# Tying scores and results to TensorE's order by halves of four heads in a gated linear attention and mixture-of-experts kernel

## The chip, the cores and the metric

The kernel runs on one core of a Trainium2 chip, in float32. The metric is the device time of one execution in microseconds (us). The kernel before takes 552.49 us (median of three runs, 552.18 to 552.93).

## What is computed

Two blocks follow one another. The first is a gated linear attention with a complex, per-channel decay; its output is laid out as 3072 rows of 384 numbers. The second sends each row to one of eight experts (two matrix products with a relu between them) and scales the result. Cut to what matters:

```
# attention: B, H, S, D = 4, 8, 768, 48
for t in range(S):
    S_re, S_im = a[t] * (S_re, S_im)  (complex)      # per-channel decay, |a| capped at 0.999
    S_re += outer(k[t], v[t])
    y[t] = q[t] @ S_re
x = y as (B*S, H*D) = (3072, 384)

# experts: E, F = 8, 1024
e = argmax(x @ w_gate)                               # one expert for a row
out = softmax weight of e * (relu(x @ w1[e]) @ w2[e])
```

## The kernel before

The attention is done in chunks of 128 time steps. There are 24 chunks: six steps in time (`s`), and for each of them the four batches (`b`). Two chunks make a unit `u`. With the sums of the logarithms of the decay and of its angles inside a chunk, the recurrence becomes matrix products. For one chunk `g`, and for each of its eight heads:

- `rotated` makes Q and K (128 time steps x 96: cosine and sine part of 48 channels) on VectorE.
- Q and K are transposed on TensorE into `tp` (PSUM, two buffers) and copied to `qt` and `kt`, by ScalarE and VectorE, four heads at a time.
- `at` = scores (128 x 128 for a head); VectorE multiplies them with the triangular mask into `am`.
- `y` = V x `am` plus (from the second time step on) carried state `G` x `qt`. These products have 64 output rows for a head. Two heads are put beside one another, `z` = 0 and `z` = 1, on the lower and the upper 64 partitions of the result.
- `dk` = K x V, what the chunk adds to the state.
- then `y` is copied, transposed (`tpx`), and the router's logits (`lt`, `lp`) are computed.

All matmuls are issued through one helper, so that the profile shows them at one line (L81); the transposes of Q and K are at L504.

```
    def scores(g):
        u, c = divmod(g, U)
        s, b = divmod(g, B)
        Q, K = rotated(u, c, "Q"), rotated(u, c, "K")
        qts, ats = [], []
        for hg in range(H // 4):                       # two halves of four heads
            kq = []
            for nm, X in (("qt", Q), ("kt", K)):
                tp = psT.tile([P, 4, P], FP, tag="tp", name="tp")
                for j in range(4):
                    nc.tensor.transpose(out=tp[0:DD, j], in_=X[:, hg * 4 + j], identity=ident)
                t = ch.tile([P, 4, P], FP, tag=nm, name=nm, bufs=4 if nm == "qt" else 2)
                copy(nm == "qt" or hg == 1, t[0:DD], tp[0:DD])     # True: ScalarE, False: VectorE
                kq.append(t)
            at = psA.tile([P, 4, P], FP, tag="at", name="at")      # one buffer
            for j in range(4):
                mm(at[:, j], kq[1][0:DD, j], kq[0][0:DD, j])
            am = ch.tile([P, 4, P], FP, tag="am", name="am", bufs=4)
            nc.vector.tensor_tensor(out=am, in0=at, in1=bc(tri, 1, 4), op=OP.mult)
            ...
        if s < CB - 1:
            dk = ...
            for h in range(H):
                mm(dk[0:DD, h], K[:, h], T["v", u][:, c, h, 0:D])

    def outputs(g):
        ...
        y = psY.tile([P, HP, P], FP, tag="y", name="y")            # one buffer
        for i in range(HP):                                        # four pairs of heads
            for z in range(2):
                hg, j = divmod(2 * i + z, 4)
                mm(y[z * DP : (z + 1) * DP, i], V[:, 2 * i + z], ats[hg][:, j], True, s == 0)
            if s > 0:
                for z in range(2):
                    hg, j = divmod(2 * i + z, 4)
                    mm(y[z * DP : (z + 1) * DP, i], G[0:DD, 2 * i + z], qts[hg][0:DD, j], False, True)
        ...                       # new state; copy of y to xt (ScalarE); transposes tpx; logits lt, lp

    for u in range(NU + 1):
        ...                       # decay and angle sums (csl, cst) of unit u
        for c in range(U):
            g = (u - 1) * U + c
            if g >= 0:
                scores(g)
            if u < NU:
                decayed(u, c)
            if g > 0:
                outputs(g - 1)    # one chunk behind the scores
            ...                   # routing
    outputs(NT - 1)
```

This text does not fix the order in which an engine executes. A scheduler orders each engine's instructions when the program is built, with the dependencies as its limits. The helper `queue(ins, before)` adds a dependency that costs no semaphore: it only fixes that `ins` comes after `before` in the order.

After the attention (at about 278 us) come the experts: for each one, `hps` = x W1, relu, `yps` = h W2.

Of the kernel before, what the change touches and what calls it, by code (L numbers as in the profile page):

```python
# [10 lines left out]
FP = mybir.dt.float32  # L11
# [3 lines left out]
OP = mybir.AluOpType  # L15
# [5 lines left out]
P = 128  # L21
# [8 lines left out]
def bc(ap, axis, n):  # L30

    shape = list(ap.shape)
    shape.insert(axis, n)
    return ap[tuple([slice(None)] * axis + [None])].to_broadcast(shape)
# [3 lines left out]
def kernel(  # L38
# [12 lines left out]
    nc = tc.nc  # L51
    B, H, S, D = q.shape
    DD = 2 * D
# [4 lines left out]
    NT = N // P  # L58
    CB = S // P
    U = 2  # L60
# [14 lines left out]
    DP = 64  # L75
    HP = H // 2
# [3 lines left out]
    def mm(o, lhsT, rhs, start=True, stop=True):  # L80
        return nc.tensor.matmul(o, lhsT=lhsT, rhs=rhs, start=start, stop=stop, skip_group_check=True)  # L81

    def copy(i, o, in_):
        (nc.scalar.copy if i % 2 else nc.vector.tensor_copy)(out=o, in_=in_)  # L84
# [7 lines left out]
    def const(shape, name, dt=FP):  # L92
        return cp.tile(shape, dt, name=name)

    ident = const([P, P], "ident")
    make_identity(nc, ident)
    tri = const([P, P], "tri")
# [21 lines left out]
    gbuf = [const([P, H, DP], f"G{i}") for i in range(B)]  # L119
# [39 lines left out]
    T, W_T = {"put": []}, {}  # L159

    def queue(ins, before):

        tc.add_manual_dep(ins.ins, before.ins.name, NOSYNC, reason="queue order")
        return ins
# [55 lines left out]
    ch = att.enter_context(tc.tile_pool(name="ch", bufs=2))  # L220
    psM = att.enter_context(tc.tile_pool(name="psM", bufs=1, space=PSUM))
    psT = att.enter_context(tc.tile_pool(name="psT", bufs=2, space=PSUM))
    psA = att.enter_context(tc.tile_pool(name="psA", bufs=1, space=PSUM))
    psY = att.enter_context(tc.tile_pool(name="psY", bufs=1, space=PSUM))
    psB = att.enter_context(tc.tile_pool(name="psB", bufs=1, space=PSUM))
    psD = att.enter_context(tc.tile_pool(name="psD", bufs=1, space=PSUM))
# [47 lines left out]
    def load_a(u):  # L274
        load(u, (("ar", a_re), ("ai", a_im)))
# [131 lines left out]
    def rotated(u, c, nm):  # L407
        t = ch.tile([P, H, 2, D], FP, tag=nm, name=nm)
        e = bc(T.pop((nm, u, c)), 2, 2)
        nc.vector.tensor_tensor(out=t, in0=T["CS", u][:, c * H : (c + 1) * H], in1=e, op=OP.mult)  # L410
        return t.rearrange("p h a d -> p h (a d)")
# [78 lines left out]

        return [lambda i=i: put(i) for i in range(n)] + ([last] if end else [])

    def scores(g):

        u, c = divmod(g, U)
        s, b = divmod(g, B)
        Q, K = rotated(u, c, "Q"), rotated(u, c, "K")
        qts, ats = [], []
        for hg in range(H // 4):
            kq = []  # L500
            for nm, X in (("qt", Q), ("kt", K)):
                tp = psT.tile([P, 4, P], FP, tag="tp", name="tp")
                for j in range(4):
                    nc.tensor.transpose(out=tp[0:DD, j], in_=X[:, hg * 4 + j], identity=ident)  # L504
                t = ch.tile([P, 4, P], FP, tag=nm, name=nm, bufs=4 if nm == "qt" else 2)
                copy(nm == "qt" or hg == 1, t[0:DD], tp[0:DD])
                kq.append(t)
            at = psA.tile([P, 4, P], FP, tag="at", name="at")
            for j in range(4):
                mm(at[:, j], kq[1][0:DD, j], kq[0][0:DD, j])  # L510
            am = ch.tile([P, 4, P], FP, tag="am", name="am", bufs=4)
            nc.vector.tensor_tensor(out=am, in0=at, in1=bc(tri, 1, 4), op=OP.mult)  # L512
            qts.append(kq[0])
            ats.append(am)
        if s < CB - 1:
            dk = psD.tile([P, H, D], FP, tag="dk", padded_shape=[P, 8, 64], name="dk")
            for h in range(H):
                mm(dk[0:DD, h], K[:, h], T["v", u][:, c, h, 0:D])
            T["dk", g] = dk
        T["s", g] = qts, ats  # L520

    def outputs(g):

        u, c = divmod(g, U)
        s, b = divmod(g, B)
        qts, ats = T.pop(("s", g))
        V, G = T["v", u][:, c], gbuf[b]
        y = psY.tile([P, HP, P], FP, tag="y", name="y")
        for i in range(HP):
            for z in range(2):  # L530
                hg, j = divmod(2 * i + z, 4)
                mm(y[z * DP : (z + 1) * DP, i], V[:, 2 * i + z], ats[hg][:, j], True, s == 0)
            if s > 0:
                for z in range(2):
                    hg, j = divmod(2 * i + z, 4)
                    mm(y[z * DP : (z + 1) * DP, i], G[0:DD, 2 * i + z], qts[hg][0:DD, j], False, True)
        if s < CB - 1:
            t = ch.tile([P, H, D], FP, tag="t", name="t")
            if s == 0:
                nc.scalar.copy(out=t[0:DD], in_=T["dk", g][0:DD])  # L540
            else:
                nc.vector.tensor_tensor(out=t[0:DD], in0=T["dk", g][0:DD], in1=G[0:DD, :, 0:D], op=OP.add)
            if b == B - 1:
                decay_total(s)
            T["t", b] = t
            if b == B - 1:
                for i in range(B):
                    M = bc(T["M", s][0:DD, i], 2, D)
                    (nc.vector.tensor_tensor(out=gbuf[i][0:DD, :, 0:D], in0=T["t", i][0:DD], in1=M, op=OP.mult))
        xt = xl.tile([P, HP, P], FP, tag="xt", name="xt")  # L550
        nc.scalar.copy(out=xt, in_=y)
        tp = psB.tile([P, HP, 2, DP], FP, tag="tp", name="tpx")
        for i in range(HP):
            nc.tensor.transpose(out=tp[:, i].rearrange("p z d -> p (z d)"), in_=xt[:, i], identity=ident)  # L554
        if b == 0:
            T["x", g] = T["x"] = xl.tile([P, GR, XW], FP, tag="x", name="x", bufs=3)
        T["copied"] = nc.scalar.copy(
            out=T["x"][:, b, :DM].rearrange("p (i z d) -> p i z d", z=2, d=D), in_=tp[:, :, :, 0:D]
        )
        logits(xt, g)  # L560
# [24 lines left out]
    for z in range(2):  # L585
        nc.sync.dma_start(
            out=wg[z * DP : z * DP + D, :, 0:E],
            in_=w_gate.rearrange("(i z d) e -> z d i e", z=2, d=D)[z],
# [14 lines left out]
    for u in range(NU + 1):  # L603
        if 0 < u < NU:
            load_qkv(u)
        for i in range(NS // (P * BL)):
            if 2 + i * 2 // (NS // (P * BL)) == u:
                blank(i)

        if u < NU:  # L610
            steps = decay_steps(u + 1)[0] if u + 1 < NU else []
            own = [lambda c=c: decay_sums(u, c) for c in range(U)]
            if u == 0:
                steps = steps[:2] + own + steps[2:]
            else:
                steps = steps[:1] + own[:1] + steps[1:3] + own[1:] + steps[3:]
            table("natural_log_exp_and_others")
            for i, f in enumerate(steps):
                f()
                if i == 1:  # L620
                    carry_angle(u)
            for f in T.pop("chosen", []):
                f()
            for c in range(U):
                angle_sums(u, c)
            table("trig_and_small")
            if 0 < u < NU - 1:
                decay_angle(u + 1)
            rotation(u)
            if u == 0:  # L630
                decay_angle(1)
            if u == NU - 1:
                while T["put"]:
                    place()
                experts_at(range(1), True)
                load_w(0, range(KD + KF // 2))
                own0 = gather(0, 0, [P] * (FIRST // P))
        if u < NU:
            place()
        for f in T.pop("route", []):  # L640
            T["put"] += f()
        for c in range(U):
            g = (u - 1) * U + c
            if g >= 0:
                scores(g)
            if u < NU:
                decayed(u, c)
            if g > 0:
                outputs(g - 1)

            n = {NT - GR: GR, NT - U: U}.get(g)
            if n:
                if n == GR:
                    queue(table("natural_log_exp_and_others"), T["copied"])
                choose(g - n, n)()
                T["put"] += route(g - n, n)
                while T["put"]:
                    place()
        for _ in range(2 if u >= NU - 2 else 1):
            place()  # L660
        if u > 2 and u % 2 and u < NU - 1:

            j = (u - 3) * U
            T["chosen"] = [choose(j, GR)]
            T["route"] = [lambda j=j: route(j, GR)]
        if u + 2 < NU:
            load_a(u + 2)
    outputs(NT - 1)
    choose(NT - U, U)()
    for f in route(NT - U, U):  # L670
# [343 lines left out]
```

## Time and profile before

| | |
|---|---|
| time, median of three | 552.49 us |
| span of the profiled execution | 551.8 us |
| TensorE busy (PE) | 535.6 us |
| VectorE busy (DVE) | 272.0 us |
| ScalarE busy (ACT) | 279.7 us |
| first matmul of the experts (hps) | 278.5 us |

In the profile PE stands for TensorE's matmuls, PEld for its weight loads, DVE for VectorE, ACT for ScalarE, POOL for GpSimd. A float32 matmul that is no transpose shows as two records of equal shape, so "x8" of `at` is four matmuls. The ends of matmuls are modelled and overlap; what a group of matmuls costs is therefore read from its start to the start of the next group.

### The profile page before, as it was taken

How to read it: one execution, taken by the hardware profiler on the slowest of the kernel's cores; microseconds unless marked ns; L12 is line 12 of the kernel's file. 1: busy time of each engine (PE TensorE's matmuls, PEld its weight loads, DVE VectorE, ACT ScalarE, POOL GpSimd, SP SyncE). 2: the span in 40 equal slices, each digit the busy share in tenths (PEclk: the TensorE clock that was granted, in tenths of full speed). 3: DMA queues.
4: the chain of work that ended last, by engine and by line, in shares of the span. 5: the costliest groups of instructions: out<-in, count | busy, mean ns of one | idle time of the engine just before them, and what ended most of it. 6: DMA issues, size and time to landing. Idle time of an engine off the chain costs nothing.

```text
span 551.8 us, 8779 instructions
## 1 busy us (share of the span) xinstructions
PE 535.6 (97%) x3310; PEld 369.7 (67%) x3310; DVE 272.0 (49%) x640; ACT 279.7 (51%) x473; POOL 128.5 (23%) x148
## 2 busy tenths in 40 slices
PE   8899999999999999999999999999999999999995
PEld 6777688778778878778776655555555555565553
DVE  3757788978888887877551212121404032210110
ACT  7867877877776886744310112534343351615200
POOL 2110111141241140210222000605234160514301
PEclk9959999999999999999999999999999999999998
DMA  9999954918754633461114996472944819370001
GB/s 186 187 259 236 262 94 88 182 52 145 129 131 88 121 84 58 105 224 18 43 44 113 309 359 160 136 194 121 281 137 163 240 47 280 128 255 15 25 4 42
DMA packets 163566, 79.32 MB, mean 144 GB/s; under 512 B 144896, under 2 KB 156861, under 8 KB 162619
## 3 DMA queue, kind: packets, MB, share of 16 engines
q1 hardware_dynamic: 158651, 69.04, 51.6%
q0 software_dynamic: 4864, 9.63, 5.0%
q8 instruction: 28, 0.46, 0.4%
q14 instruction: 23, 0.19, 0.1%
HBM read 63.30 MB, written 15.46 MB: 143 GB/s over the span
## 4 chain that ended last, share of the span: by engine, by line
PE 84%; DMA 6%; DVE 3%; ACT 3%; issue 3%; SPq 0%; POOL 0%; POOLq 0%; DVEq 0%; ACTq 0%
PE hps L81 23%; PE yps L81 22%; PE y L81 9%; PE at L81 7%; PE tp L504 7%; PE dk L81 5%; PE cst L81 3%; PE csl L81 3%; DMA ai<-in_a_im_dram 2%; PE tpx L554 2%; DMA xs<-x,slot 1%; PE lt L81 1%; DMA ai<-c 1%; DMA c<-ai 1%; ACT R L230 1%
## 5 line engine op out<-in xcount | busy, mean ns | idle before, releaser
L81 PE MATMUL yps<-w2t,ht 128*128 128x384 f32 (+6 forms) x464 | 135.1, 487 | 0.0
L81 PE MATMUL hps<-xt,w1t 128*128 128x256 f32 (+8 forms) x432 | 133.9, 469 | 0.3 <-DVE xt L708 0.3
L81 PEld LDWEIGHTS hps<-xt,w1t 128*128 128x128 f32 x432 | 80.0, 190 | 52.8 <-issue 25.2
L81 PEld LDWEIGHTS yps<-w2t,ht 128*128 128x128 f32 (+6 forms) x464 | 75.8, 177 | 56.8 <-issue 6.9
L742 ACT ACTIVATE ht<-hps 128x256 f32<-128x256 f32 (+8 forms) x36 | 17.0, 472 | 118.5 <-PE hps L81 117.5
L759 DVE TENSOR_SCALAR y<-yps,gi 128x384 f32<-128x384 f32 (+2 forms) x24 | 14.7, 615 | 107.6 <-PE yps L81 107.6
L722 POOL DMA_INDIRECT out_dram<-y,gi x29 | 28.2, 974 | 122.6 <-DVE y L759 86.5
L81 PE MATMUL at<-qt,kt 96*128 96x128 f32 x384 | 54.9, 286 | 0.9 <-DVE kt L84 0.9
L746 DVE TENSOR_SCALAR ht<-hps 128x256 f32<-128x256 f32 (+8 forms) x36 | 19.2, 532 | 70.9 <-PE hps L81 70.8
L81 PEld LDWEIGHTS at<-qt,kt 96*128 96x128 f32 x384 | 48.7, 196 | 6.5 <-DVE kt L84 1.4
L81 PE MATMUL y<-am,v 128*64 128x128 f32 x384 | 52.8, 288 | 0.0
L81 PE MATMUL y<-qt,G 96*64 96x128 f32 x320 | 45.5, 280 | 0.0
L482 POOL DMA_INDIRECT xs<-x,slot x24 | 24.8, 1035 | 86.2 <-DMA xs<-x,slot 39.8
L81 PEld LDWEIGHTS y<-am,v 128*64 128x64 f32 x384 | 32.7, 137 | 13.7 <-issue 12.3
L512 DVE TENSOR_TENSOR am<-at,tri 128x512 f32<-128x512 f32 x48 | 33.0, 687 | 13.9 <-PE at L81 13.4
L84 ACT COPY qt<-tp 96x512 f32<-96x512 f32 x48 | 27.9, 581 | 15.1 <-PE tp L504 15.0
L242 ACT ACT_TABLE_LOAD x27 | 34.6, 1283 | 1.2 <-PEq L1000 0.8
L504 PE MATMUL tp<-ident,Q 128*96 128x128 f32 x192 | 32.5, 285 | 2.0 <-DVE Q L410 2.0
L800 POOL TENSOR_TENSOR cs<-cs,cw 128x768 f32<-128x768 f32 x12 | 21.7, 1809 | 50.7 <-ACT cw L796 50.7
L81 PEld LDWEIGHTS dk<-v,K 128*96 128x96 f32 x320 | 31.4, 170 | 3.0 <-issue 1.9
L504 PE MATMUL tp<-ident,K 128*96 128x128 f32 x192 | 32.5, 283 | 0.7 <-DVE K L410 0.7
L81 PEld LDWEIGHTS y<-qt,G 96*64 96x64 f32 x320 | 30.9, 136 | 3.2 <-issue 2.6
(140 smaller groups left out, 752.8 us busy)
## 6 DMA issues: line engine op xcount, KB each, us to landing
w1t<-in_moe_w_dram SPq DMA_DIRECT2D x7, 1536.0 KB, 7.1
w2t<-in_moe_w_dram SPq DMA_DIRECT2D x7, 1536.0 KB, 7.5
xs<-zrow SPq DMA_DIRECT2D x7, 772.0 KB, 10.3
q<-in_q_dram SPq DMA_DIRECT2D x12, 384.0 KB, 5.3
k<-in_k_dram SPq DMA_DIRECT2D x12, 384.0 KB, 5.5
v<-in_v_dram SPq DMA_DIRECT2D x12, 384.0 KB, 4.3
car<-in_a_re_dram SPq DMA_DIRECT2D x12, 384.0 KB, 8.3
cai<-in_a_im_dram SPq DMA_DIRECT2D x12, 384.0 KB, 9.2
```

The costliest lines, as they stand in the source:

```text
L81: return nc.tensor.matmul(o, lhsT=lhsT, rhs=rhs, start=start, stop=stop, skip_group_check=True)
L84: (nc.scalar.copy if i % 2 else nc.vector.tensor_copy)(out=o, in_=in_)
L242: ins = nc.scalar.preload_act_table_set(name)
L482: pool(nc.gpsimd.indirect_dma_start(out=xs[:, :], out_offset=bass.IndirectOffsetOnAxis(ap=to[:, i : i + 1], axis=0), in_=x[:, i], in_offse ...
L504: nc.tensor.transpose(out=tp[0:DD, j], in_=X[:, hg * 4 + j], identity=ident)
L512: nc.vector.tensor_tensor(out=am, in0=at, in1=bc(tri, 1, 4), op=OP.mult)
L554: nc.tensor.transpose(out=tp[:, i].rearrange("p z d -> p (z d)"), in_=xt[:, i], identity=ident)
L722: T["out"] = nc.gpsimd.indirect_dma_start(out=out, out_offset=bass.IndirectOffsetOnAxis(ap=idx, axis=0), in_=y[0:m], in_offset=None, bound ...
L742: relu = nc.scalar.activation(out=ht[:, f], in_=ps, func=AF.Relu)
L746: nc.vector.tensor_scalar(out=ht[:, f], in0=ps, scalar1=0.0, scalar2=None, op0=OP.max)
L759: nc.vector.tensor_scalar(out=y[0:m], in0=ps[0:m], scalar1=gate, scalar2=None, op0=OP.mult)
L800: nc.gpsimd.tensor_tensor(out=s, in0=s, in1=w, op=OP.add)
```

## The change

`scores` is cut into `turned` (rotation once for a chunk, and the transposes and copies of one half of four heads), `scores` (score products and mask of one half) and `update` (the products `dk`). The matmuls of the result move out of `outputs` into `results`, which does one half of four heads. All matmuls of `turned`, `scores` and `results` go through `pe`, which ties each one behind the one before it in TensorE's order; the others (`csl`, `cst`, `dk`, `tpx`, `lt`, `lp`) stay free for the scheduler to put between them. The two halves of the result of chunk g-1 now stand among the pieces of chunk g. The purpose is to give TensorE other work in each place where it would have to wait for a copy or a mask, and to keep each piece together.

```diff
+    def pe(ins):
+        if "pe" in T:
+            queue(ins, T["pe"])
+        T["pe"] = ins
+
+    def turned(g, hg):
+        u, c = divmod(g, U)
+        if hg == 0:
+            T["QK", g] = rotated(u, c, "Q"), rotated(u, c, "K")
+        kq = []
+        for nm, X in zip(("qt", "kt"), T["QK", g]):
+            tp = psT.tile([P, 4, P], FP, tag="tp", name="tp")
+            for j in range(4):
+                pe(nc.tensor.transpose(out=tp[0:DD, j], in_=X[:, hg * 4 + j], identity=ident))
+            ...                                   # copies as before
+        T["kq", g, hg] = kq
+
+    def scores(g, hg):
+        qt, kt = T["kq", g, hg]
+        at = psA.tile([P, 4, P], FP, tag="at", name="at")
+        for j in range(4):
+            pe(mm(at[:, j], kt[0:DD, j], qt[0:DD, j]))
+        ...                                       # mask as before
+    def update(g):
+        ...                                       # dk as before, not tied
+    def results(g, hg):
+        ...
+        if hg == 0:
+            T["y"] = psY.tile([P, HP, P], FP, tag="y", name="y")
+        y, am, qt = T["y"], T["am", g, hg], T["kq", g, hg][0]
+        for i in range(2):
+            for z in range(2):
+                o = y[z * DP : (z + 1) * DP, 2 * hg + i]
+                pe(mm(o, V[:, 4 * hg + 2 * i + z], am[:, 2 * i + z], True, s == 0))
+            if s > 0:
+                for z in range(2):
+                    o = y[z * DP : (z + 1) * DP, 2 * hg + i]
+                    pe(mm(o, G[0:DD, 4 * hg + 2 * i + z], qt[0:DD, 2 * i + z], False, True))
 ...
             if g >= 0:
-                scores(g)
+                turned(g, 0)
+            if g > 0:
+                results(g - 1, 0)
+            if g >= 0:
+                turned(g, 1)
+                scores(g, 0)
+                update(g)
+            if g > 0:
+                results(g - 1, 1)
+            if g >= 0:
+                scores(g, 1)
             if u < NU:
                 decayed(u, c)
             if g > 0:
                 outputs(g - 1)
 ...
+    for hg in range(H // 4):
+        results(NT - 1, hg)
     outputs(NT - 1)
```

No product, copy or mask is added or left out, and no buffer changes.

More of the change, by code (lines that the diff above doesn't have):

```diff
@@ L491, in route @@
         return [lambda i=i: put(i) for i in range(n)] + ([last] if end else [])
-    def scores(g):
+    def pe(ins):
[11 more added lines that the diff above has]
+                pe(nc.tensor.transpose(out=tp[0:DD, j], in_=X[:, hg * 4 + j], identity=ident))
+            t = ch.tile([P, 4, P], FP, tag=nm, name=nm, bufs=4 if nm == "qt" else 2)
+            copy(nm == "qt" or hg == 1, t[0:DD], tp[0:DD])
+            kq.append(t)
+        T["kq", g, hg] = kq
@@ new lines, in scores @@
+    def scores(g, hg):
[3 more added lines that the diff above has]
+            pe(mm(at[:, j], kt[0:DD, j], qt[0:DD, j]))
+        am = ch.tile([P, 4, P], FP, tag="am", name="am", bufs=4)
+        nc.vector.tensor_tensor(out=am, in0=at, in1=bc(tri, 1, 4), op=OP.mult)
+        T["am", g, hg] = am
+    def update(g):
+        u, c = divmod(g, U)
+        if g // B < CB - 1:
+            dk = psD.tile([P, H, D], FP, tag="dk", padded_shape=[P, 8, 64], name="dk")
+            for h in range(H):
+                mm(dk[0:DD, h], T["QK", g][1][:, h], T["v", u][:, c, h, 0:D])
+            T["dk", g] = dk
@@ L495, in scores @@
+    def results(g, hg):
         u, c = divmod(g, U)
         s, b = divmod(g, B)
[L497 to L520, printed above, removed]
+        V, G = T["v", u][:, c], gbuf[b]
+        if hg == 0:
[9 more added lines that the diff above has]
+                    pe(mm(o, G[0:DD, 4 * hg + 2 * i + z], qt[0:DD, 2 * i + z], False, True))
@@ L525, in outputs @@
         s, b = divmod(g, B)
[L526 to L536, printed above, removed]
+        y, G = T["y"], gbuf[b]
         if s < CB - 1:
```

## The prediction

> **What bounds the kernel now.** I begin with the page: its busy row of TensorE, and the chain of work that ended last.
>
> ```profile
> PE 535.6 (97%) x3310; PEld 369.7 (67%) x3310; DVE 272.0 (49%) x640; ACT 279.7 (51%) x473; POOL 128.5 (23%) x148
> ...
> PE 84%; DMA 6%; DVE 3%; ACT 3%; issue 3%; SPq 0%; POOL 0%; POOLq 0%; DVEq 0%; ACTq 0%
> ```
>
> TensorE is busy nearly everywhere and has 84% of the chain. The change touches the attention only, so I ask next from when on TensorE is that stage's bound. The chain in order of time shows it:
>
> ```profile
> 57.04 4.42 issue
> 61.47 0.01 POOLq L389
> 61.48 4.71 DMA c<-ai
> 66.19 0.02 issue
> 66.22 0.16 DVE c L327
> 66.38 0.87 DVE Q L410
> 67.25 0.88 DVE K L410
> 68.13 0.04 issue
> 68.17 0.64 PE tp L504 x4
> ```
>
> Columns are start, length, what. Until 68 us the chain runs over loads, the carried angle and VectorE. From 68.17 us it stays on TensorE, with one short detour, until the experts start at 278.5 us. TensorE time saved before 68 us therefore doesn't reach the end; time saved in the 209 us from 68 to 277 us does. In that stretch the table of windows (busy time of each engine) and TensorE's waits say:
>
> ```profile
> sum 209.00, PE 205.58 PEld 163.16 DVE 168.34 ACT 146.79 POOL 41.29; mean PE 41.12 PEld 32.63 DVE 33.67 ACT 29.36 POOL 8.26
> ```
>
> ```profile
> PE tpx L554 <- ACT xt L551: 1.3, 4, 0.7
> PE cst L81 <- DMA ai<-c: 0.8, 1, 0.8
> PE cst L81 <- DVE f L381: 0.6, 1, 0.6
> PE at L81 <- DVE kt L84: 0.5, 1, 0.5
> PE tp L504 <- DVE K L410: 0.2, 1, 0.2
> ```
>
> Idle time of TensorE is 209.0 - 205.6 = 3.4 us, and its waits sum to 3.4 us. So the waits that the change is meant to fill are worth 3.4 us at most. A larger gain would have to come from TensorE doing the same work in less time, and for that the timeline of TensorE is the view to read:
>
> ```profile
> 194.75 0.49 PE L504 MATMUL tp<-ident,Q 128*96 128x128 f32 x3
> 195.08 0.60 PE L504 MATMUL tp<-ident,K 128*96 128x128 f32 x4
> 195.61 0.43 PE L81 MATMUL y<-am,v 128*64 128x128 f32 x2
> 195.98 0.64 PE L504 MATMUL tp<-ident,Q 128*96 128x128 f32 x4
> 196.55 0.32 PE L81 MATMUL y<-am,v 128*64 128x128 f32 x1
> ...
> 197.14 1.16 PE L81 MATMUL at<-qt,kt 96*128 96x128 f32 x8
> 198.13 0.81 PE L81 MATMUL cst<-ai,tri_turn 128*128 128x384 f32 x2
> ```
>
> From start to start: three transposes take 195.08 - 194.75 = 0.33 us, 0.11 each. The next four, 0.44 us by that, take 0.53 before a `y` starts: about 0.1 us goes into entering `y`. One lone `y` matmul (two records) takes 0.37 us, where its passes need 2 x 0.107 = 0.21: about 0.16 us goes into leaving. The run at 196.55 takes 0.59 us for four matmuls: two pairs, each pair side by side in the time of one (0.21), plus 0.16 again. So a `y` matmul has three costs: its share of a pair, the entering and leaving of its run, and, if its partner isn't beside it, half a pair's time for nothing.
>
> [...]
>
> **The change part by part.** The same 3310 matmuls are issued; no copy, mask or transfer is added or taken away. What moves is the order. I take it from the instruction orders of the two built programs, by counting unbroken runs of `y` matmuls.
>
> - *Runs.* Before there are 81 `y` runs with 352 matmuls, some as short as one; after there are 60, of which 28 hold exactly the eight matmuls of a half. From the first decay total on (the eight small `mt` transposes, at 69 us before), where savings count: 70 runs before, 53 after, 17 fewer. At 0.10 + 0.16 = 0.26 us each, 17 x 0.26 = 4.4 us.
> - *Broken pairs.* A run with an odd number of matmuls leaves one without a partner, which costs 0.107 us. In the same part 40 runs are odd before and 24 after: 16 x 0.107 = 1.7 us. Together 6.1 us. As a cross-check I summed all 70 runs of the timeline from 68 to 277 us, from a run's first start to the next foreign start: 50.3 us. The 324 matmuls in perfect pairs need 162 x 0.215 = 34.8 us. The remaining 15.5 us are 0.22 for a run; with a mean 0.15 us of entering (the same reading over all entries) a run costs 0.37 us, and 17 x 0.37 = 6.3 us. The two ways agree, so I take 6.2 us.
> - *Other borders.* Transposes stand in 99 runs before and 77 after, but a border between two kinds that use the full width costs some 0.05 us (score products after transposes: 0.046 us, the median of ten such borders). Most of the missing borders are those of `y`, counted already. 0.5 us.
> - *The old waits.* 1.3 us of the 3.4 us are for the copy of `y` before `tpx`, which now has a half's scores (four at 0.215, 0.86 us) ahead of it; the copy takes 0.58 us. I take 0.5 us off.
> - *New waits.* Here the fixed order can cost. `at` has one buffer. Between the scores of the two halves stands, at the least, one half of results: four pairs, 0.86 us, and 0.26 us of borders, 1.12 us in all. The mask takes 0.69 us, plus about 0.2 us for signals either way, an estimate. That leaves 0.2 us if VectorE is free, but it is busy 168.3 of 209 us and many of its operations take 0.55 to 0.95 us. When one has just started, TensorE waits up to 0.7 us. In the new order `dk`, `csl` or `cst` stand in that gap in some chunks, not in all. I take 0.12 us for each of 20 chunks, 2.4 us. The second half's transposes need the `tp` buffers of the first half: the VectorE copy (0.69 us) has the 1.12 us of results and another 0.43 us of Q's transposes before it is missed, so I add nothing.
>
> The sum: -6.2 - 0.5 - 0.5 + 2.4 = -4.8 us. The early part (four fewer runs before 68 us) adds nothing, since its chain isn't TensorE's. The experts move as a whole: their first input (`xt`) is complete at 264.7 us, 14 us before its use, so the start at 278.5 us is bound by TensorE. 552.5 - 4.8 = 547.7; I predict 547.5 us.
>
> **The rivals.** *First, the new order waits.* Tied matmuls can't be passed by other tied ones, so one late mask or copy stops all three kinds; before, the scheduler could place whatever it thought was ready. For it: VectorE's and ScalarE's shares of 81% and 70%, and the one `at` buffer. Against it: the waits of before are only 3.4 us though the same buffers were used, and six kinds of matmul stay free. If each chunk waited 0.35 us instead of 0.12, 20 x 0.35 = 7 us would cancel the gain: 552 us; at 0.5 us, 555 us.
>
> *Second, another path becomes the bound.* The carried angle goes through two small transfers and GpSimd's queue (1.7 to 5.4 us to landing), and the one detour of the chain after 68 us is this path, with 0.8 us of TensorE waiting. If TensorE gets ahead by 5 us, such a wait may reach 2 to 3 us once or twice, since the last angle transfer is issued behind a row scatter [...]. The result would be 550 us. Against it: the path has two units, about 40 us, for its round.
>
> *Third, the borders are worth more than I count.* Modelled ends hide waits inside "busy" time, and if whole runs of eight also shorten the borders among the rest, a run could be worth 0.5 us: 17 x 0.5 + 1.7 = 10.2 us. With few new waits that gives 542 to 543 us.
>
> **Range and chances.** The middle case is 547.5 us. The first rival sets the upper end at 552.5 us, the third the lower at 542.5 us. Two per cent is 11 us: faster than 541.4 us needs the third rival with no new wait at all, 0.06. Slower than 563.5 us needs 0.9 us of new wait in every chunk, which the few waits of before speak against, 0.03. Within: 0.91.
>
> **What the profile after would show.** The time from `y` start to the next foreign start, summed from 68 us on, should fall from 50.3 us to about 44 us, with some 53 runs. The first matmul of the experts should come near 273.5 us, and the time from there to the end should stay at 273.3 us. TensorE's idle time in the attention should rise to about 5 us, with `at` waiting for `am`. I am wrong if `y` keeps its time although its runs are whole (then the borders aren't the cost), if waits of the tied matmuls grow beyond 6 us, or if the experts' part changes its length.

## The result, and the profile after

The changed kernel takes 557.5 us (median of four runs, 556.99 to 558.23) against 552.67 us before: a ratio of 1.0089, with a 95% interval of 1.0072 to 1.0107. It is 4.8 us slower. The prediction was 5 us faster, with 552.5 us as the upper end of its range. Four slow executions in the runs below, of 562.28, 573.25, 593.56 and 1351.33 us, are left out of the medians.

The same two lines of the page, after:

```profile
PE 530.2 (96%) x3310; PEld 370.6 (67%) x3310; DVE 271.5 (49%) x640; ACT 280.5 (51%) x473; POOL 136.6 (25%) x148
...
PE 82%; ACT 5%; DVE 4%; DMA 4%; issue 3%; POOL 1%; SPq 0%; POOLq 0%; DVEq 0%; ACTq 0%
```

TensorE is busy 5.4 us less, as the better order promises, but the span is 3.3 us longer. So TensorE stands idle for longer somewhere. To find where, cut both executions at two events that both have: the first decay total (the eight `mt` transposes after the first time step's chunks) and the first matmul of the experts. The table of windows, first before, then after; columns are the stretch, its length, and the busy time of each engine (PE, PEld, DVE, ACT, POOL), then the mean clock that TensorE was granted (1.00 is full speed), the busy share of the DMA engines and their GB/s:

```profile
20.00:69.36 49.36, 45.54 (x330) 34.49 (x329) 34.14 (x58) 39.01 (x61) 5.51 (x11) 0.86 1.17 245
69.36:278.47 209.11, 205.33 (x1961) 162.93 (x1959) 167.04 (x408) 146.16 (x252) 41.61 (x57) 1.00 0.48 103
```

```profile
20.00:76.28 56.28, 44.78 (x319) 34.84 (x317) 34.89 (x58) 39.43 (x62) 5.47 (x10) 0.85 1.03 221
76.28:282.33 206.05, 200.03 (x1970) 162.16 (x1968) 165.64 (x407) 146.26 (x252) 50.34 (x57) 1.00 0.49 103
```

The main stretch became 209.11 - 206.05 = 3.1 us shorter, although nine more matmul records (some 1 us of work, an estimate at the 205.33 us / 1961 = 0.105 us of a record in the first table) now lie in it. The early stretch became 56.28 - 49.36 = 6.9 us longer. The experts' part is the same, 273.3 us and 272.8 us. The whole loss lies before the first `mt`, in the part to which the prediction gave zero.

What happens there is seen in TensorE's waits from 24 to 90 us of the changed kernel (who waited for whom; total, times, longest):

```profile
PE tp L508 <- DVE Q L410: 4.7, 2, 2.9
PE at L81 <- DVE am L521: 3.9, 1, 3.9
```

Of these, 1.75 us at 24.7 us are there before the change too. New are a stop of 2.9 us ahead of 47.19 us (with 0.7 us for K right after it) and one of 3.9 us ahead of 70.28 us. Both times VectorE is late. Its own timeline shows why, here at the second stop:

```profile
64.00 0.56 DVE L384 TENSOR_SCALAR fa<-f 128x768 int32<-128x768 int32 x1
69.38 0.16 DVE L327 SCALAR_TENSOR_TENSOR c<-fl,c 96x8 f32<-96x8 f32 x1 [4.81 <-DMA c<-ai]
69.46 0.68 DVE L521 TENSOR_TENSOR am<-at,tri 128x512 f32<-128x512 f32 x1
70.06 0.94 DVE L410 TENSOR_TENSOR Q<-CS,Qe 128x768 f32<-128x768 f32 x1
```

A tiny operation, the addition of the carried angle (`c`, 96 x 8 numbers, 0.16 us), waits 4.8 us for its transfer. The mask `am` and the rotation of Q stand behind it in VectorE's order and start only after it, at 69.46 and 70.06 us. TensorE needs both. The waits of VectorE for this transfer, from 24 to 90 us, before and then after:

```profile
DVE c L327 <- DMA c<-ai: 4.2, 2, 2.5
```

```profile
DVE c L327 <- DMA c<-ai: 9.2, 2, 4.8
```

The transfers themselves were not quicker before: 8.6 us from issue to landing for the first and 4.7 us for the second, against 7.7 and 6.7 us. But VectorE's order was another one. At both places the mask of the latest scores stood ahead of the addition before, and stands behind it after. The second place before the change:

```profile
63.81 0.69 DVE L512 TENSOR_TENSOR am<-at,tri 128x512 f32<-128x512 f32 x1 [0.19 <-PE at L81]
66.22 0.16 DVE L327 SCALAR_TENSOR_TENSOR c<-fl,c 96x8 f32<-96x8 f32 x1 [1.71 <-DMA c<-ai]
```

So TensorE had scores and results to do meanwhile, and lost only 0.2 to 0.4 us at each place. At the second place of the changed kernel nothing is recorded on VectorE in the 4.81 us, though the scores that the mask reads were done at 64.93 us (start 63.87 us, length 1.06 us), 4.5 us before the mask started.

A second cost follows each stop. Windows of the changed kernel; the third column from the right is the granted clock:

```profile
45.00:50.00 5.00, 2.11 (x14) 1.65 (x16) 3.66 (x7) 2.98 (x6) 0.51 (x1) 0.81 1.03 210
50.00:55.00 5.00, 5.00 (x27) 3.88 (x24) 3.14 (x5) 0.45 (x1) 0.00 (x0) 0.50 0.65 128
...
65.00:70.00 5.00, 1.36 (x10) 0.57 (x8) 0.62 (x2) 3.02 (x4) 0.00 (x0) 0.86 1.04 254
70.00:75.00 5.00, 4.72 (x27) 4.00 (x28) 3.43 (x5) 1.65 (x4) 0.51 (x1) 0.50 1.18 226
```

In the 5 us after each stop TensorE is busy nearly all the time, but at half its clock (27 matmul records in the first of these stretches; 45 or 46 in the same stretches at full clock, shown further below). The stops ahead of them took 2.9 + 0.7 us and 3.9 us.

Another stretch at half clock stands beside shorter waits, and hides a part of the loss. It begins near 26 us before the change and near 28 us after, ahead of both stops. The windows from 25 to 40 us, before and then after:

```profile
25.00:30.00 5.00, 4.03 (x16) 2.67 (x17) 5.00 (x7) 4.27 (x7) 0.00 (x0) 0.58 1.39 201
30.00:35.00 5.00, 5.00 (x28) 4.93 (x27) 2.17 (x4) 3.06 (x6) 1.14 (x2) 0.50 1.30 201
35.00:40.00 5.00, 5.00 (x24) 3.15 (x23) 1.43 (x3) 4.02 (x5) 0.54 (x1) 0.55 1.11 321
```

```profile
25.00:30.00 5.00, 3.63 (x20) 2.56 (x18) 4.62 (x7) 3.46 (x6) 0.00 (x0) 0.77 1.40 203
30.00:35.00 5.00, 4.42 (x31) 3.63 (x31) 2.50 (x5) 3.66 (x7) 1.12 (x2) 0.89 1.37 203
35.00:40.00 5.00, 5.00 (x49) 4.32 (x48) 3.76 (x7) 4.27 (x6) 0.54 (x1) 1.00 1.07 338
```

It comes after a wait of 1.76 us that ends at 25.04 us before the change, and one of 1.75 us that ends at 24.67 us after it; two shorter ones (0.23 and 0.70 us before, 0.22 and 1.15 us after) lie near its start. In the kernel before it goes on through 11 us in which TensorE is recorded as busy throughout. No run here shows what sets its length. The missing clock is (0.42 + 0.50 + 0.45) x 5 = 6.9 us before and (0.23 + 0.11) x 5 = 1.7 us after. By this estimate the profiled execution of the changed kernel lost some 5 us less there, so the new stops and the half clock behind them cost more than the 6.9 us by which the early stretch grew.

### The profile page after: what moved, and what is told of

Its sections match the earlier page's. It is cut to its first block, busy times and chain, and to the rows that moved or that the text cites. A ratio compares the mean times of both kernels' runs of the same rounds, so it can differ in the third digit from the quotient of the medians.

```text
span 555.1 us, 8777 instructions
## 1 busy us (share of the span) xinstructions
PE 530.2 (96%) x3310; PEld 370.6 (67%) x3310; DVE 271.5 (49%) x640; ACT 280.5 (51%) x473; POOL 136.6 (25%) x148
## 4 chain that ended last, share of the span: by engine, by line
PE 82%; ACT 5%; DVE 4%; DMA 4%; issue 3%; POOL 1%; SPq 0%; POOLq 0%; DVEq 0%; ACTq 0%
PE yps L81 24%; PE hps L81 24%; PE y L81 7%; PE tp L508 7%; PE at L81 7%; PE dk L81 4%; DMA c<-ai 3%; PE csl L81 2%; PE cst L81 2%; PE tpx L572 2%; ACT R L230 2%; ACT L242 1%; PE lt L81 1%; PE lp L81 1%; DMA ar<-in_a_re_dram 1%
## 5 line engine op out<-in xcount | busy, mean ns | idle before, releaser
L482 POOL DMA_INDIRECT xs<-x,slot x24 | 33.2, 1382 | 76.9 <-DMA xs<-x,slot 36.9
L81 PE MATMUL y<-am,v 128*64 128x128 f32 x384 | 43.1, 289 | 0.0
L81 PE MATMUL y<-qt,G 96*64 96x128 f32 x320 | 35.5, 274 | 0.0
L508 PE MATMUL tp<-ident,K 128*96 128x128 f32 x192 | 31.3, 283 | 2.1 <-DVE K L410 1.4
L81 PE MATMUL dk<-v,K 128*96 128x48 f32 x320 | 32.3, 253 | 0.0
L81 PEld LDWEIGHTS y<-am,v 128*64 128x64 f32 x384 | 24.5, 137 | 10.2 <-issue 7.8
```

The lines of the kernel that those rows point to most:

```text
L482: pool(nc.gpsimd.indirect_dma_start(out=xs[:, :], out_offset=bass.IndirectOffsetOnAxis(ap=to[:, i : i + 1], axis=0), in_=x[:, i], in_offse ...
L508: pe(nc.tensor.transpose(out=tp[0:DD, j], in_=X[:, hg * 4 + j], identity=ident))
```

## The experiments

Theory 1: VectorE's queue is blocked by the one instruction that waits for the angle's transfer, and the new order made that hit TensorE. Theory 2: the tie itself, which forbids TensorE to do other tied work, makes the stops. Theory 3: the clock falls in the early part whatever is done.

**The addition of the angle on GpSimd**, in the changed kernel and in the kernel before (`twopi` is a constant tile that holds 2 pi):

```diff
-            nc.vector.scalar_tensor_tensor(
-                out=c0, in0=T["fl", u - B // U], scalar=2.0 * math.pi, in1=c0, op0=OP.mult, op1=OP.add
-            )
+            fl = T["fl", u - B // U]
+            nc.gpsimd.tensor_tensor(out=fl, in0=fl, in1=twopi, op=OP.mult)
+            nc.gpsimd.tensor_tensor(out=c0, in0=fl, in1=c0, op=OP.add)
```

> The changed kernel with the carried angle added by GpSimd (two small operations) instead of by VectorE, so that VectorE's queue no longer waits for the small transfer. Theory 1 (VectorE stands behind a transfer, and TensorE behind VectorE): the two stops of TensorE at 44 to 49 us and 66 to 70 us and the half clock after each vanish, some 10 to 12 us less than the changed kernel: 545 to 548 us. Theory 2 (the tied order itself stops TensorE in the early chunks): within 2 us of the changed kernel, 556 to 558 us. Theory 3 (the clock falls in the early part whatever stands there): clock low at 50 to 55 and 70 to 75 us still, gain at most 5 us.

> The kernel before with the same move of the carried angle from VectorE to GpSimd. Theory 1: the kernel before had small stops from it (VectorE idle 2.5 and 1.7 us, TensorE 0.2 us), so 0 to 3 us less, 550 to 552.5 us, and the changed kernel with the same move stands 4 to 7 us below it. Theory 2: no change for either, 552.5 us.

Measured: 546.9 us and 549.8 us; ratios to the kernel before of 0.987 (0.980 to 0.994) and 0.9935 (0.991 to 0.996). Both stops are gone. The changed kernel now is the faster of the two, by 2.9 us, less than the 4 to 7 us expected: a wait of 2.2 us of `cst` came in at 54.68 us. The profile records no releaser for it, but GpSimd took 3.05 us for one addition and sent the angle back only at 50.55 us, which would explain it. GpSimd's timeline of the changed kernel with this move (start, length, what, idle before it and its releaser):

```profile
47.21 3.05 POOL L331 TENSOR_TENSOR c<-fl,c 96x8 f32<-96x8 f32 x1 [5.22 <-DMA c<-ai]
```

**The zero fill one unit later.** In those microseconds the buffer that will hold the routed rows is filled with zeros, 5.4 MB in seven transfers of 772 KB and a small one.

```diff
-            if 2 + i * 2 // (NS // (P * BL)) == u:
+            if 3 + i * 2 // (NS // (P * BL)) == u:
```

> The changed kernel with the zero fill of the row buffer issued one unit later (units 3 and 4 instead of 2 and 3); everything else as it is. Theory 1 with the fill as the cause of the slow transfer: the carried angle's first transfer lands in 3 to 4 us instead of 7.7, the first stop of TensorE (2.9 us) shrinks below 1 us and so does the clock loss after it; the second stays or moves to the next unit. In all 2 to 6 us less: 551 to 555 us. Theory 2: no change, 557 us.

Measured: 554.23 us, ratio 1.0014 (0.999 to 1.004), some 3 us less than the changed kernel. The first transfer was issued at 36.98 us, and VectorE made the addition at 40.31 us without a recorded wait, 3.3 us later; in the changed kernel 38.41 and 46.10 us, 7.7 us. The first stop vanished. The second is there as before, 4.4 us; four of the transfers now fall beside it. TensorE's waits in this kernel:

```profile
PE at L81 <- DVE am L521: 4.8, 2, 4.4
```

So the transfer of 3 KB took 7.7 us here with the zero fill issued just ahead of it, and 3.3 us without. The loads of the next unit move with the fill, so their share is not separated.

**Idle matmuls in the stops.**

```diff
+            if (g, hg, nm) == (2, 0, "qt"):
+                for i in range(14):
+                    pe(mm(tp[:, 0], ident, ident))
...
+        if (g, hg) == (3, 1):
+            o = psB.tile([P, HP, P], FP, tag="tp", name="fill")
+            for i in range(18):
+                pe(mm(o[:, 0], ident, ident))
```

> The changed kernel with 14 and 18 idle matmuls added in TensorE's order just ahead of the two points at which it stops (the first transposes of chunk 2 and the second scores of chunk 3). The stops stay as long as they are, but TensorE is busy in them. If the half clock after a stop is a cost of its own, caused by TensorE standing idle, it goes and the time falls by 3 to 5 us to 552 to 554 us. If the clock falls for another cause, the time stays at 557 us or rises by up to 1 us.

Measured: 558.14 us (553.67 to 560.56). In the profiled execution, the one of 553.67 us, the clock is 1.00 from 44 to 78 us. It is 1.00 from 20 to 44 us as well, so the earlier stretch at half clock is missing too. The other five took 557.57 us or more at a mean clock of 0.979 to 0.983 over the execution (0.996 in the profiled one), and no trace shows where they lost it. This does not settle how much of the loss is the half clock.

**No tie for the chunks before chunk 5.**

```diff
-        if "pe" in T:
-            queue(ins, T["pe"])
-        T["pe"] = ins
+        if T.get("tie"):
+            if "pe" in T:
+                queue(ins, T["pe"])
+            T["pe"] = ins
...
+            T["tie"] = g >= 5
```

> The changed kernel with the tie in TensorE's order taken off for the chunks before chunk 5, so that the scheduler is free there as before; the order of the code stays in halves. Theory 2 (the tie stops TensorE early): 545 to 550 us. Theory 1 (VectorE's queue): the stops stay, since VectorE's order is as it was: 555 to 558 us.

Measured: 549.81 us, ratio 0.9941 (0.990 to 0.998). That is the number of theory 2, and theory 1's number failed. VectorE still waits 4.1 and 2.5 us for the transfers; TensorE's first stop is 2.54 us, its second 0.85 us. Its timeline:

```profile
43.91 0.65 PE L81 MATMUL y<-am,v 128*64 128x128 f32 x6
...
47.78 0.64 PE L509 MATMUL tp<-ident,Q 128*96 128x128 f32 x4 [2.54 <-DVE Q L410]
...
66.61 1.13 PE L81 MATMUL at<-qt,kt 96*128 96x128 f32 x8 [0.85 <-DVE am L522]
```

Results of chunk 1 are computed at 43.91 us, ahead of the transposes that wait. In the changed kernel the tie puts them behind these transposes, though their inputs are ready, and they run at 49.67 us. So the tie does keep work out of that stop, but the stop is only 0.4 us shorter without it. At the second stop the transfer took 3.9 us in place of 6.7 us, and VectorE goes on at 65.70 us, against 69.38 us. That is 3.7 us earlier, and the stop is 3.1 us shorter: the earlier landing covers it. This run does not separate the tie from the transfer.

**The addition kept on VectorE, but behind its rotations and masks.**

```diff
-            nc.vector.scalar_tensor_tensor(
+            ins = nc.vector.scalar_tensor_tensor(
                 out=c0, in0=T["fl", u - B // U], scalar=2.0 * math.pi, in1=c0, op0=OP.mult, op1=OP.add
             )
+            for w in T["behind"]:
+                queue(ins, w)
...                                # ahead of unit u's decay: Q and K of the next chunk, their last
+        if u * U >= B and u < NU:  # rotation and the last mask go into T["behind"]
+            T["QK", (u - 1) * U] = rotated(u - 1, 0, "Q"), rotated(u - 1, 0, "K")
+            T["behind"] = [T["rot"], T["mask"]]
```

> The changed kernel with the carried angle's addition kept on VectorE but tied behind the rotations of the next chunk and the masks before it, so that VectorE has served TensorE before it waits for the transfer. Theory 1 (one instruction's place in VectorE's queue is the cause): the two stops of 2.9 and 3.9 us and the clock loss behind them vanish as with GpSimd, without GpSimd's slow operation: 543 to 547 us. If only the move to GpSimd helped for another reason: 555 us or more.

> The kernel before with the same tie of the carried angle's addition. Theory 1: 548 to 552 us, and the distance to the changed kernel with this tie is the pure worth of the new TensorE order: 4 to 7 us by the borders of the result's runs.

Measured: 555.17 us and 557.10 us; ratios 1.0027 (1.000 to 1.005) and 1.0071 (1.004 to 1.010). My expectation failed for both. The early stops did vanish. But the addition was now late in every unit, and later in the attention the sums of the angles had to wait for it, 5.6 us at once in the changed kernel. TensorE's waits there, after 90 us:

```profile
PE cst L81 <- DMA ai<-c: 5.6, 1, 5.6
```

**Only the first two additions behind** (`if u in (2, 3)` in place of `if u * U >= B and u < NU`, and `T.pop("behind", [])` in place of `T["behind"]`), where the transfers meet the zero fill. The changed kernel unaltered ran on the same chip.

> The changed kernel with only the first two of the carried angle's additions (units 2 and 3, where the transfers meet the zero fill) tied behind VectorE's rotations and masks; the later ones stay where the scheduler put them. Theory 1: no stop of TensorE over 1 us at 44 to 49 or 66 to 70 us, and no late wait for the angle: 544 to 549 us, 8 to 12 us below the changed kernel as it is. If the late waits of the fully deferred kernel come from something else, they stay and the time is near 555 us.

> The kernel before with the same two additions tied. Its stops at these places were small: 550 to 554 us. The distance to the changed kernel with the two ties is the worth of the new order from the borders and pairs of the result matmuls: 4 to 7 us by the prediction.

> The changed kernel unaltered, on the same chip as the other three, so that they can be compared directly: 556 to 559 us, some 4 us above the kernel before; both theories expect the same.

Measured: 544.75 us for the changed kernel with the two ties, ratio 0.9865 (0.984 to 0.989); 549.54 us for the kernel before with them, 0.9937 (0.992 to 0.996); 556.85 us for the changed kernel unaltered, 1.0089 (1.006 to 1.012). The place of two instructions of 0.16 us in VectorE's order is worth 12.1 us in the changed kernel and 2.5 us in the kernel before (552.08 us there; all differences of medians). Of the 2.5 us only some 0.8 us are waits (TensorE's from 40 to 70 us fell from 1.2 to 0.4 us). In the profiled executions the half clock that begins ahead of 28 us was also over sooner with the ties, at 35 us instead of 39.5 us. That the ties did this is not shown. VectorE's timeline and the windows of the changed kernel with the ties:

```profile
62.12 0.69 DVE L523 TENSOR_TENSOR am<-at,tri 128x512 f32<-128x512 f32 x1
62.73 0.95 DVE L412 TENSOR_TENSOR K<-CS,Ke 128x768 f32<-128x768 f32 x1
63.99 0.16 DVE L327 SCALAR_TENSOR_TENSOR c<-fl,c 96x8 f32<-96x8 f32 x1 [0.32 <-DMA c<-ai]
```

```profile
50.00:55.00 5.00, 5.00 (x45) 3.69 (x44) 4.93 (x9) 4.55 (x9) 1.15 (x2) 1.00 0.71 122
...
70.00:75.00 5.00, 5.00 (x46) 3.83 (x45) 4.69 (x7) 4.33 (x7) 0.35 (x1) 1.00 0.80 128
```

The addition waits 0.32 us, with the mask and the rotations done, and the half clock at these two places is gone too. The transfers are as slow as ever, 6.7 and 7.0 us from issue to addition; only the addition's place in VectorE's order has changed. Theory 3 is out for them. Where the stops are away, 7.5 us of TensorE's waits are away (2.9 + 0.7 + 3.9); the other 4.6 of the 12.1 us fit the two stretches at half clock, but were not measured by themselves. With these ties the new order is worth 549.54 - 544.75 = 4.8 us.

**The results in four pieces a chunk instead of two**, first on the fully deferred kernel, then on the one with two ties. Each half of `results` is cut at `i`; the second part is put after the Q transposes or in the middle of the scores:

```diff
-                turned(g, 1)
+                turned(g, 1, (lambda: results(g - 1, 0, (1,))) if g > 0 else None)
...
-                scores(g, 1)
+                scores(g, 1, (lambda: results(g - 1, 1, (1,))) if g > 0 else None)
```

> The changed kernel with the deferred addition, and each half of the results cut in two pieces of four matmuls (two in the first time step) with transposes or scores put between: 106 runs of result matmuls in TensorE's order instead of 63, no product added. If a border pair costs the 0.26 us read from the timeline, 43 more runs give 11 us more than with the deferred addition alone (with 0.37 us 16 us): 555 to 562 us. If borders are free: the same time within 2 us.

> The changed kernel with the two ties and each half of the results cut in two pieces, transposes or scores between them: 100 runs of result matmuls instead of 61. At 0.26 to 0.37 us for a run, 39 runs give 10 to 14 us more than the kernel with the two ties alone, and more only if TensorE's waits grow; borders free: within 2 us.

Measured: 587.89 us, ratio 1.058 (1.049 to 1.068), for the first. It can't be read for the borders: `cst` waits 9.3 us for the angle, and the mean clock is 0.91 from 90 to 180 us. The second took 558.45 us, 13.7 us more than with two pieces. From 20 us to the first matmul of the experts it takes 264.0 us against 250.5 us: 13.5 us for 39 runs. Of that, 2.0 us are longer idle time of TensorE (11.4 against 9.4 us; one wait of 3.4 us of `cst` came in). A part of the rest is clock, 0.96 over the last 95 us, which is worth at most 3.8 us. So a run costs between 0.20 and 0.29 us, where the prediction took 0.26 us.

## Why the prediction was wrong

*The step that failed* is the sentence on the early part: "The early part (four fewer runs before 68 us) adds nothing, since its chain isn't TensorE's." The reasoning was one-sided. Saved TensorE time did not help there, but the order could still harm: the chain hung on transfers and VectorE, and the order decided how much TensorE had left to do while they were late, and which instruction of VectorE stood behind a late transfer. In place of zero the runs showed +6.9 us up to the first `mt`. Two ties on VectorE took away those stops and 12.1 us, while the tied order of TensorE stayed.

*The second rival* named the right path, the carried angle, but in the wrong place and size: one or two waits of 2 to 3 us after 68 us, because TensorE would be ahead. They came before, and VectorE brought them to TensorE. The kernel before had shown it: in the chain lines that the prediction prints, the transfer of 4.71 us is followed by the addition and then by Q and K on VectorE. I read these lines only for when TensorE becomes the bound. And the 1.7 to 5.4 us to landing that the prediction gives are those of the stretch after 68 us; the transfer issued at 39 us in the kernel before took 8.6 us.

*The first rival* said that one late mask stops all tied kinds. That is the 3.9 us stop, once and not in every chunk. With the addition out of the way the stop is gone although all ties stand, so the tie alone does not make it. Without the early ties the time fell to 549.81 us, but there the transfer landed earlier; how much of the stop a free order would have filled is not shown.

*The steady part* held. The sum of -4.8 us is to be set beside the -4.8 us of the two kernels with the ties, and their main stretches: 205.56 us against 210.36 us. As it stands, the change shortened the main stretch by 3.1 us, or some 4 us with the nine records that moved into it. The runs were 70 and 53, as counted. Their time, read as in the prediction with waits left out, fell from 50.2 to 46.2 us, 4.0 us, where the prediction said that it would fall by 6.2 us to about 44 us. That was a slip of reading: entering a run lies ahead of its first start and so outside this time. By the prediction's own costs only 17 x 0.16 + 1.7 = 4.4 us could show in it. What runs and broken pairs cost separately was not measured, and what makes a border cost time, or keeps a broken pair apart, was not shown. The 0.2 us for signals between scores and mask can be read: 0.03 to 0.05 us from the end of the scores to the mask where VectorE waits for them, and 0.14 and 0.16 us from the end of the mask to the scores at the changed kernel's two waits for `am` (70.28 and 261.23 us). The new waits came to about what was set for them, but not where: TensorE's idle time in the stretch went from 3.8 to 6.0 us, 2.2 us more (1.9 us net in the sum), and only 0.4 us of its waits are for `am`; the others are single waits of `csl`, `cst` and transposes. Of the old waits for `xt`, 2.0 us in this stretch, 0.7 us is left.

*The clock* was not in the prediction at all, though the profile of the kernel before shows 0.50 to 0.58 of full speed from 25 to 40 us. In the changed kernel each of the two stops, of 2.9 + 0.7 us and 3.9 us, had some 5 us at half clock behind it.

## What to carry to other kernels

Before reordering the bound engine, look in the queues of the engines that feed it for an instruction that waits on a transfer, and see what stands behind it: a cheap instruction can be an expensive one by its place (two of 0.16 us were worth 12.1 us here). A stage whose chain isn't the bound engine's may gain nothing from a faster order (with the two ties the early stretch took 45.0 us in the new order and 44.7 us in the old), but can lose by it (6.9 us in the changed kernel as it stands), so it needs its own reading. Of a set of ties, keep those that save borders; leaving free the work that can fill a wait is a guess that the kernel without the early ties suggests and does not prove.

## What the hardware showed that I had not expected

- A transfer of 3 KB took 3.3 us from issue to use where the DMA engines were nearly idle for 1.5 us of it (37.5 to 39.0 us, the zero fill one unit later), and 7.7 us just after 3.1 MB of zero fill had been issued, with loads beside it.
- GpSimd took 3.05 us for one addition of 96 x 8 numbers, and 0.21 us for the multiplication of the same size that followed it at 51.08 us (spans on GpSimd are rough in the profile).
- Stops of 2.9 + 0.7 us and of 3.9 us were each followed by some 5 us at half clock. Beside a wait of 1.75 us and two shorter ones lay 3.4 us of it in the changed kernel, 13.7 us in the kernel before, and none in the profiled execution with the idle matmuls.
